# Halved products in the routing of an attention and mixture-of-experts kernel, with its scatters and remainders moved

## The chip, the cores and the metric

One core of one Trainium2 chip runs the whole kernel. The metric is the device time of one execution in microseconds (us); of several executions the median is taken, and less is better. TensorE, VectorE, ScalarE, GpSimd and the DMA queues are PE, DVE, ACT, POOL and SP in the rows.

## What is computed

Linear attention feeds a mixture of experts with one expert a token. Of the reference the parts that matter here:

```python
q_p, k_p = phi(q_s), phi(k_s)                 # exp(h - max(h)), 128 features
kv = np.einsum('bhsm,bhsd->bhmd', k_p, v)     # key sums of a batch
num = np.einsum('bhsm,bhmd->bhsd', q_p, kv)
...
logits = xn @ en.T / tau
expert_idx = np.argmax(logits, axis=1)        # one of 8 experts
...
h = np.maximum(x[mask] @ w1[e], 0.0)
out[mask] = gate_w[mask, None] * (h @ w2[e])
```

There are 8 batches of 576 tokens, 8 heads of 64 numbers, and experts of 512 x 1024 and 1024 x 512 weights.

## The kernel before, in words

The first part, some 210 us, makes attention and routing; the second, the rest, runs 38 steps of 128 tokens through the experts. The change lies in the first part.

Tokens are 36 tiles of 128. A loop (L746) runs over i: it takes keys of tile i and, seven behind, queries of tile i-7, in one round. The order of instructions on every engine is written out by hand (manual_schedule); small jobs are put into named slots of a round (early, spare, mid, ends) and taken out by go() and slot(). In a full round:

- TensorE projects the queries (proj, L374), turns the last tile's query features (qtr, L462) into both banks of tile nuu, projects the keys, adds the keys' products to the key sums (kvmm, L406, one half), makes the numerators (num, L482) into nuu, and adds the other half of kvmm.
- ScalarE copies one half of the turned queries (qcopy, L467) and takes exponentials (feats, L388).
- VectorE copies the other half (qcopy, L469), takes maxima (L378), and reads the numerators out of nuu (num_out, L495 to L501); the next qtr writes nuu only behind that.

nuu is one PSUM tile of two banks of 512 columns; nu[0] and nu[1] are views of it. The numerators use columns 0 to 291 of each bank, the expert logits of the key sums 424 to 487 of the second, the counting products 424 to 455 of the first.

Twice in nine rounds the key sums of a batch are ready (u in 4, 8). Then GpSimd packs them (kv_dense, L424), and two rounds later TensorE turns them (kv_turn, L433, slot spare 3, right ahead of num), VectorE copies them back (kv_turned, L437, slot mid 4), and TensorE multiplies them with the expert embeddings (kv_logits, L444, slot spare 0, right behind num). In the full rounds the turn goes into bank pb[3].

After every third tile routed() handles three tiles: logits are summed, the best expert chosen (sel, L530 to L532, VectorE), tokens before each token counted by products of sel with a triangle and with ones (L537, L539, TensorE), rows worked out (L548 to L558, GpSimd), and the three tiles scattered into expert order (L570, an indirect DMA from GpSimd, one a round, held behind L501 of its round). A table, plan, says in which slot each step stands.

From round 29 on the first expert's weights come in eight pieces; first_split (L608, L610) rounds a piece, and first_rest (L617) subtracts to keep the remainder, on GpSimd.

Of the kernel before, what the change touches and what calls it, by code (L numbers as in the profile page):

```python
# [11 lines left out]
F32 = mybir.dt.float32  # L12
# [5 lines left out]
ALU = mybir.AluOpType  # L18
# [4 lines left out]
P = 128  # L23
B, H, S, D, M = 8, 8, 576, 64, 128
E, F = 8, 1024
# [4 lines left out]
NTILE = NSB * TPS  # L30
G = 3
# [18 lines left out]
SHIFTW = 8  # L50
BESIDE = 554
WARM = 28
FILL1, FILL2, FILL3 = 2, 4, 5
NSTAT = 38
NSTEP = 64
# [9 lines left out]
def attention_moe(ctx: ExitStack, tc: tile.TileContext, qT, kT, v1, omT, emb, tau, w1q, w2q, xs, out):  # L65
    nc = tc.nc
    sync = mybir.DependencyInfo(mybir.DependencyClass.Sync, mybir.DependencyReason.DATA)
# [8 lines left out]
    nuu = ps.tile([P, 2, 512], F32, name="nuu")  # L76
    nu = [nuu[:, a] for a in range(2)]
    pb = [ps.tile([P, 512], F32, name=f"pb{a}") for a in range(4)]
# [9 lines left out]
    one16 = const.tile([P, P], BF16, name="one16")  # L88
# [4 lines left out]
    ident = const.tile([P, P], F32, name="ident")  # L93
    make_identity(nc, ident)

    tri = const.tile([P, P], BF16, name="tri")
# [5 lines left out]
    iotm = const.tile([P, E], F32, name="iotm")  # L102
# [220 lines left out]
    with ExitStack() as c1:  # L323
# [5 lines left out]
        kva, kvs, st = {}, {}, {}  # L329
# [98 lines left out]

        def kv_turn(sb, b):
            kvc = st["kvc", sb, b]  # L430
            st["kvb"] = bank = pb[3] if st["both"] and (sb, b) != (0, 0) else nu[1]
            for c in range(4):
                nc.tensor.transpose(bank[:, c * P : (c + 1) * P], kvc[:, 2 * c : 2 * c + 2, :].rearrange("p a d -> p (a d)"), ident)  # L433

        def kv_turned(sb, b):
            kvt = xgp[NPRE][:, 0:DM].rearrange("p (c m) -> p c m", c=4)
            nc.vector.tensor_copy(kvt.rearrange("p c m -> p (c m)"), st["kvb"])  # L437
            st["kvt", sb, b] = kvt

        def kv_logits(sb, b):  # L440
# [23 lines left out]
        def qcopy(i, s, on_act=False):  # L464
            st["qp", i, s] = qp = p1.tile([P, H, D], F32, name=f"qp{i}_{s}", tag="ftk" if s and not st["both"] and i >= NTILE - LAG else "qp", bufs=3)
            if on_act:
                o = nc.scalar.activation(qp, st["tr", i][s], AF.Copy)  # L467
            else:
                o = nc.vector.tensor_copy(qp, st["tr", i][s])  # L469
            if ("cp", i) in st:  # L470
                tc.declare_no_dep(o.ins, st["cp", i].ins.name, reason="reads the other bank")
            st["cp", i] = o
# [33 lines left out]
        def routed(g):  # L506

            bc = lambda a: a.unsqueeze(2).to_broadcast([P, G, E])
            ibc = lambda a: a.unsqueeze(1).to_broadcast([P, G, E])
            new = lambda n, shape, dt=F32: small.tile(shape, dt, name=f"{n}{g}", tag=n, bufs=1 if n in ("t4", "base") else 2)  # L510
            raw = new("raw", [P, G, E])
            mx = new("mx", [P, G])
            sel = sels[g % 2][:, 0:G]
            lg = st["lg", g]
            fast = g >= NTILE // G - 3
            if fast:
                nc.vector.tensor_reduce(raw, lg.rearrange("p g h e -> p g e h"), axis=AX.X, op=ALU.add)
            else:
                pt = nc.gpsimd.tensor_tensor
                t4 = new("t4", [P, G, 4, E])  # L520
                pt(t4, lg[:, :, 0:4], lg[:, :, 4:8], op=ALU.add)
                pt(t4[:, :, 0:2], t4[:, :, 0:2], t4[:, :, 2:4], op=ALU.add)
                pt(raw, t4[:, :, 0], t4[:, :, 1], op=ALU.add)
            yield
            nc.vector.tensor_reduce(mx, raw, axis=AX.X, op=ALU.max)
            nc.vector.tensor_tensor(raw, raw, bc(mx), op=ALU.subtract)
            yield
            for j in range(G):
                nc.gpsimd.tensor_copy(st["xr", g * G + j][:, DM : DM + E], raw[:, j])
            nc.vector.scalar_tensor_tensor(sel, raw, 0.0, ibc(iotm), op0=ALU.is_ge, op1=ALU.mult)  # L530
            nc.vector.tensor_reduce(mx, sel, axis=AX.X, op=ALU.min)
            nc.vector.tensor_tensor(sel, ibc(iotm), bc(mx), op=ALU.is_equal)  # L532
            yield

            bank, o = nu[0], 424
            pr = bank[:, o : o + (G + 1) * E].rearrange("p (j e) -> p j e", e=E)
            nc.tensor.matmul(pr, tri, sels[g % 2], start=True, stop=False)  # L537
            for j in range(G):
                nc.tensor.matmul(pr[:, j + 1 :], one16, sel[:, j : j + 1].to_broadcast([P, G - j, E]), start=False, stop=j == G - 1)  # L539
            yield  # L540
            base = new("base", [P, G + 1, E])
            rows = base[:, 0:G]
            if fast:
                nc.vector.tensor_tensor(rows, pr[:, 0:G], run.unsqueeze(1).to_broadcast([P, G, E]), op=ALU.add)
                nc.vector.tensor_tensor(run, run, pr[:, G], op=ALU.add)
            else:
                nc.vector.tensor_copy(base, pr)
                pt(rows, rows, run.unsqueeze(1).to_broadcast([P, G, E]), op=ALU.add)  # L548
                pt(run, run, base[:, G], op=ALU.add)
            pos = new("pos", [P, G, 4])  # L550
            if fast:
                nc.vector.tensor_tensor(rows, rows, sel, op=ALU.mult)
                nc.vector.tensor_reduce(pos[:, :, 0], rows, axis=AX.X, op=ALU.add)
            else:
                pt(rows, rows, sel, op=ALU.mult)
                pt(pos, rows[:, :, 0:4], rows[:, :, 4:8], op=ALU.add)
                pt(pos[:, :, 0:2], pos[:, :, 0:2], pos[:, :, 2:4], op=ALU.add)
                pt(pos[:, :, 0:1], pos[:, :, 0:1], pos[:, :, 1:2], op=ALU.add)  # L558
            yield
            if g == GPICK:  # L560
                yield from pick_first()

            posi = new("posi", [P, G], I32)
            (nc.vector if fast else nc.gpsimd).tensor_copy(posi, pos[:, :, 0])
            for j in range(G):
                yield
                if j == 0 and g in DRAINS:
                    tc.add_manual_dep(nc.gpsimd.drain().ins, st["out"].ins.name, sync, reason="idle behind the last scatter")
                xr = st["xr", g * G + j]
                w = nc.gpsimd.indirect_dma_start(  # L570
                    out=xs, out_offset=bass.IndirectOffsetOnAxis(ap=posi[:, j : j + 1], axis=0),
                    in_=xr, in_offset=None, bounds_check=ROWS - 1, oob_is_err=False,
                )
                tc.add_manual_dep(w.ins, st["out"].ins.name, sync, reason="one scatter a tile")
                written(w)

        def pick_first():
# [34 lines left out]
        def first_rest(n):  # L612
            q, (_, h, l) = n // 2, W[("w1", "w2")[n % 2]]
            raw = st["rf", n]
            for c in range(0, F, 256):
                c = slice(c, c + 256)
                nc.gpsimd.tensor_tensor(l[:, 0, q, c], raw[:, c], h[:, 0, q, c].bitcast(F32), op=ALU.subtract)  # L617

        def first_steps():

# [125 lines left out]
        for i in range(NTILE + LAG + 2):  # L746
# [133 lines left out]
            if sums and done % G == G - 1:  # L880
                g = done // G
                steps = routed(g)
                if g == GPICK:
                    plan = [(ends, i), (mid, i + 1, 2), (mid, i + 1, 1), (spare, i + 2, 0), (mid, i + 2, 0)]
                    plan += [(mid, i + 3, 2), (mid, i + 3, 1)] + [(ends, i + 3 + k) for k in range(3)]
                elif g == NTILE // G - 2:
                    plan = [(ends, i), (ends, i + 1), (ends, i + 1), (spare, i + 2, 0), (mid, i + 2, 0), (mid, i + 2, 1)]
                    plan += [(ends, i + 2), (ends, i + 3), (ends, i + 3)]
                elif i >= NTILE:
                    plan = [(ends, i)] * 3 + [(spare, i + 1, 0), (mid, i + 1, 0), (mid, i + 1, 1)]  # L890
                    plan += [(ends, i + 2 + k) for k in range(3)]
                else:
                    plan = [(ends, i), (mid, i + 1, 2), (mid, i + 1, 1), (spare, i + 2, 0), (mid, i + 2, 0)]
                    plan += [(mid, i + 3, 2)] + [(ends, i + 3 + k) for k in range(3)]
                if NTILE - 3 < i < NTILE:
                    plan[-3:] = [(ends, i + 3), (mid, i + 4, 3), (ends, i + 5)]
                for n, (d, *key) in enumerate(plan):
                    todo = at(d, *key) if key[0] < NTILE + LAG + 2 else behind
                    todo.insert(0 if n == 0 else len(todo), (next, steps, None))
# [468 lines left out]
```

## Time and profile before

| | us |
|---|---|
| median of 3 runs | 635.08 |
| the runs | 635.08, 634.54, 641.2 |
| the profiled execution | 639.0 |
| its span | 637.4 |

Granted TensorE clock of the profiled execution: 0.998 of full speed. The profile is of one execution, so sums of its durations stand against 639.0, of which 1.6 lie around the span. A row of the timeline merges equal instructions that follow each other: its second number runs from the start of the first to the end of the last. Ends of matmuls are modelled. Idle time in square brackets stands before the instruction, with what ended it.

### The profile page before, as it was taken

To read this page: it belongs to the slowest core of one execution; us is meant where nothing else is said; L and a number is where in the kernel's file an instruction comes from. 1 tells how busy PE (TensorE), PEld (TensorE's weight loads), DVE (VectorE), ACT (ScalarE), POOL (GpSimd) and SP (SyncE) were. 2 spreads that over 40 slices of the span, in tenths; PEclk is the share of its full clock that TensorE was granted. 3 is DMA by queue.
4 is the path that set the end of the run, shared out by engine and by line. 5 is a ranking of instruction groups with operands and counts; after the bars stand their busy time and mean duration, and the time that the engine had idled before them with its cause. 6 is when DMAs were issued, how large, how long until landed. Compare 5 with 4: busy or idle time off the path is not lost.

```text
span 637.4 us, 19063 instructions
## 1 busy us (share of the span) xinstructions
PE 626.5 (98%) x6289; PEld 534.8 (84%) x6290; DVE 499.4 (78%) x909; ACT 434.5 (68%) x1143; POOL 423.1 (66%) x603
## 2 busy tenths in 40 slices
PE   9999999999999999999999999999999999999996
PEld 8999999988878787888888888888888888888885
DVE  5788888898879846789888798877778787878754
ACT  6989898898998417666666666666575757576640
POOL 3013333455777644569897898879797988797952
PEclk9999999999999999999999999999999999999999
DMA  7755665777782278888869687887878786968631
GB/s 256 216 153 170 210 197 177 226 206 235 250 284 87 101 236 296 249 214 242 244 193 230 208 225 231 201 248 185 242 186 222 216 242 196 234 206 225 195 116 47
DMA packets 143264, 132.20 MB, mean 207 GB/s; under 512 B 107766, under 2 KB 107894, under 8 KB 143168
## 3 DMA queue, kind: packets, MB, share of 16 engines
q1 hardware_dynamic: 136544, 109.96, 61.4%
q0 software_dynamic: 6480, 20.91, 8.4%
q8 instruction: 57, 0.93, 0.6%
q14 instruction: 39, 0.32, 0.2%
q10 hardware_dynamic: 144, 0.07, 0.0%
HBM read 83.78 MB, written 21.97 MB: 166 GB/s over the span
## 4 chain that ended last, share of the span: by engine, by line
PE 70%; ACT 2%; DVE 1%; DMA 1%; issue 0%; POOL 0%; ACTq 0%
PE pb L285 31%; PE po L285 31%; PE pb L374 2%; PE fs_o L285 2%; PE nuu L482 2%; PE fs_a L285 1%; PE pb L267 1%; ACT ftq L388 1%; PE kva L406 1%; DMA qt<-qT 1%; PE pb L462 0%; PE nuu L462 0%; ACT sq L296 0%; DVE xr L501 0%; DVE rt_p L299 0%
## 5 line engine op out<-in xcount | busy, mean ns | idle before, releaser
L240 POOL TENSOR_TENSOR w2l<-raww,w2h 128x256 f32 x128 | 143.6, 1122 | 7.6
L240 POOL TENSOR_TENSOR w1l<-raww,w1h 128x256 f32 (+1 forms) x130 | 114.9, 884 | 14.6 <-DMA xgp<-xs 5.3
L285 PE MATMUL po<-w2h,hh 128*128 (+1 forms) x288 | 112.2, 390 | 0.0
L285 PE MATMUL po<-w2h,hl 128*128 (+1 forms) x288 | 112.1, 389 | 0.0
L285 PE MATMUL po<-w2l,hh 128*128 (+1 forms) x288 | 112.0, 389 | 0.0
L285 PE MATMUL pb<-w1h,xh 128*128 (+1 forms) x280 | 109.4, 391 | 0.1
L285 PE MATMUL pb<-w1h,xl 128*128 (+1 forms) x280 | 109.1, 390 | 0.0
L285 PE MATMUL pb<-w1l,xh 128*128 (+1 forms) x280 | 109.0, 389 | 0.0
L1086 DVE COPY pl<-pb 128x512 uint16<-128x512 uint16 x68 | 46.7, 690 | 55.9 <-ACT pl L1082 53.0
L1082 ACT ACTIVATE pl<-pb 128x512 uint16<-128x512 uint16 x68 | 39.4, 582 | 69.5 <-PE pb L285 61.1
L388 ACT ACTIVATE ftq<-pb,nmq 128x128 f32<-128x128 f32 x288 | 79.7, 432 | 2.2 <-DVE nmq L378 2.2
L388 ACT ACTIVATE ftk<-pb,nmk 128x128 f32<-128x128 f32 x272 | 76.6, 492 | 4.9 <-DVE nmk L378 4.9
L315 POOL DMA_INDIRECT y<-xgp,tail x36 | 44.6, 1240 | 52.0 <-DVE w1h L234 25.3
L1104 DVE COPY wd<-t 128x1024 uint16<-128x1024 uint16 x68 | 67.3, 991 | 1.6 <-DMA t<-pl 1.5
L1120 ACT ACTIVATE hh<-wd 128x1024 fp32r<-128x1024 f32 x34 | 36.1, 1062 | 42.1 <-DVE wd L1104 37.4
L285 PEld LDWEIGHTS po<-w2h,hh 128*128 128x128 f32 x288 | 54.1, 188 | 11.3
L285 PEld LDWEIGHTS po<-w2h,hl 128*128 128x128 f32 x288 | 54.0, 187 | 11.3
L285 PEld LDWEIGHTS po<-w2l,hh 128*128 128x128 f32 x288 | 54.1, 188 | 11.0
L285 PEld LDWEIGHTS pb<-w1h,xl 128*128 128x128 f32 x280 | 52.6, 188 | 11.2 <-DVE xl L269 0.2
L285 PEld LDWEIGHTS pb<-w1h,xh 128*128 128x128 f32 x280 | 52.5, 187 | 11.1 <-ACT tail L1148 0.5
L285 PEld LDWEIGHTS pb<-w1l,xh 128*128 128x128 f32 x280 | 52.6, 188 | 10.8
L1124 DVE SCALAR_TENSOR_TENSOR hl<-wd,hh 128x1024 fp32r<-128x1024 f32 x34 | 54.8, 1611 | 2.9 <-ACT hh L1120 2.3
(342 smaller groups left out, 1257.2 us busy)
## 6 DMA issues: line engine op xcount, KB each, us to landing
raww<-w1q SPq DMA_DIRECT2D x38, 512.0 KB
raww<-w2q SPq DMA_DIRECT2D x38, 512.0 KB
qt<-qT SPq DMA_DIRECT2D x36, 256.0 KB
kt<-kT SPq DMA_DIRECT2D x35, 256.0 KB
xg<-xs SPq DMA_DIRECT2D x23, 260.5 KB
xgp<-xs SPq DMA_DIRECT2D x15, 260.5 KB
rf<-w1q SPq DMA_DIRECT2D x4, 512.0 KB
rf<-w2q SPq DMA_DIRECT2D x4, 512.0 KB
```

The lines of the kernel that those rows point to most:

```text
L240: ils.append(eng.tensor_tensor(at(l, d)[:, c], raw[:, c], at(h, d)[:, c].bitcast(F32), op=ALU.subtract))
L267: nc.tensor.transpose(bank[:, c * P : (c + 1) * P], src[:, o + c * P : o + (c + 1) * P], ident)
L285: done.append(nc.tensor.matmul(dst, x[:, c * P : (c + 1) * P], ws.rearrange("p o f -> p (o f)"), start=(begin and i == 0 and k == 0), stop ...
L315: w = nc.gpsimd.indirect_dma_start(out=out, out_offset=bass.IndirectOffsetOnAxis(ap=(xg[:, DM:] if tail is None else tail)[:, E : E + 1].b ...
L374: nc.tensor.matmul(st["pj" + w, i, a][:, c, :], st[w, i][r, c, :], om[r, :], start=True, stop=True)
L388: nc.scalar.activation(ft[:, h, :], pj[:, h, :], AF.Exp, bias=nm[:, h : h + 1])
L482: nc.tensor.matmul(pn[a][s * D : s * D + D, h, :], st["qp", i, s][:, 2 * h + a, :], kvs[sb, int(u > 4 - s)][:, 4 * a + h, :], start=True, ...
L1082: nc.scalar.activation(planes[1][:, o : o + 512], halved(src)[:, :, 1], AF.Copy)
L1086: nc.vector.tensor_copy(planes[0][:, o : o + 512], halved(src)[:, :, 0])
L1104: nc.vector.tensor_copy(to, src)
L1120: nc.scalar.activation(hh, wd[:, 0:F], AF.Relu)
L1124: nc.vector.scalar_tensor_tensor(hl, wd[:, 0:F], 0.0, hh.bitcast(F32), op0=ALU.max, op1=ALU.subtract)
```

## The change

It has four parts. The turns of key sums (kv_turn) are made of two 64-row halves, eight products of 64 columns for four of 128; one half goes into pb[3], the other into columns 296 to 423 of both banks of nuu (in the first and the last turn into nu[0] and nu[1]), and VectorE copies them in two copies. The counting products are made for 64 tokens' rows at a time, eight for four. A scatter in a full round is held behind VectorE's query copy (moved) and stands in slot mid 4 of the round after. The first remainder of each piece of weights is held behind the last choice of experts (sel).

```diff
+SPARE = 296
...
         def kv_turn(sb, b):
             kvc = st["kvc", sb, b]
-            st["kvb"] = bank = pb[3] if st["both"] and (sb, b) != (0, 0) else nu[1]
+            two = nuu[:, :, SPARE : SPARE + P].rearrange("p k (c r) -> p k c r", r=64)
+            if st["both"] and (sb, b) != (0, 0):
+                one = pb[3][:, 0 : 2 * P].rearrange("p (k c r) -> p k c r", c=2, r=64)
+            else:
+                one, two = (b[:, 0 : 2 * P].rearrange("p (k c r) -> p k c r", c=2, r=64) for b in nu)
+            st["kvb"] = one, two
             for c in range(4):
-                nc.tensor.transpose(bank[:, c * P : (c + 1) * P], kvc[:, 2 * c : 2 * c + 2, :].rearrange("p a d -> p (a d)"), ident)
+                for s, to in enumerate((one, two)):
+                    r = slice(64 * s, 64 * s + 64)
+                    nc.tensor.transpose(to[:, c // 2, c % 2], kvc[r, 2 * c : 2 * c + 2, :].rearrange("p a d -> p (a d)"), ident[r, r])
 
         def kv_turned(sb, b):
             kvt = xgp[NPRE][:, 0:DM].rearrange("p (c m) -> p c m", c=4)
-            nc.vector.tensor_copy(kvt.rearrange("p c m -> p (c m)"), st["kvb"])
+            for s, got in enumerate(st["kvb"]):
+                nc.vector.tensor_copy(kvt.rearrange("p (k c) (s r) -> p s k c r", k=2, r=64)[:, s], got)
...
-                o = nc.vector.tensor_copy(qp, st["tr", i][s])
+                o = st["moved"] = nc.vector.tensor_copy(qp, st["tr", i][s])
...
-            nc.vector.tensor_tensor(sel, ibc(iotm), bc(mx), op=ALU.is_equal)
+            st["sel"] = nc.vector.tensor_tensor(sel, ibc(iotm), bc(mx), op=ALU.is_equal)
...
-            nc.tensor.matmul(pr, tri, sels[g % 2], start=True, stop=False)
+            half = [slice(c, c + 64) for c in range(0, P, 64)]
+            for r in half:
+                nc.tensor.matmul(pr[r], tri[:, r], sels[g % 2], start=True, stop=False)
             for j in range(G):
-                nc.tensor.matmul(pr[:, j + 1 :], one16, sel[:, j : j + 1].to_broadcast([P, G - j, E]), start=False, stop=j == G - 1)
+                for r in half:
+                    nc.tensor.matmul(pr[r, j + 1 :], one16[:, r], sel[:, j : j + 1].to_broadcast([P, G - j, E]), start=False, stop=j == G - 1)
...
-                tc.add_manual_dep(w.ins, st["out"].ins.name, sync, reason="one scatter a tile")
+                tc.add_manual_dep(w.ins, st["moved" if st["both"] else "out"].ins.name, sync, reason="one scatter a tile")
...
-                nc.gpsimd.tensor_tensor(l[:, 0, q, c], raw[:, c], h[:, 0, q, c].bitcast(F32), op=ALU.subtract)
+                o = nc.gpsimd.tensor_tensor(l[:, 0, q, c], raw[:, c], h[:, 0, q, c].bitcast(F32), op=ALU.subtract)
+                if c.start == 0:
+                    tc.add_manual_dep(o.ins, st["sel"].ins.name, sync, reason="not beside the choice of experts")
...
+                for k in range(3):
+                    if i + 4 + k < NTILE:
+                        plan[k - 3] = (mid, i + 4 + k, 4)
```

On TensorE, in a round that turns key sums (kva are the key sums' products, xgp the packed sums, nuu behind them the numerators), the order before is:

```order
L406 MATMUL kva_0_1_887<-vt10v,ftk_1_928 64x65 x7
L433 MATMUL pb_74<-ident,xgp_141 128x128 [waits DVE_49,Activation_49,Pool_49]
L433 MATMUL pb_74<-ident,xgp_141 128x128 x3
L482 MATMUL nuu<-kvs_0_440,qp_0_980 64x73 [waits DVE_49]
L482 MATMUL nuu<-kvs_0_440,qp_1_978 64x73
```

and after:

```order
L407 MATMUL kva_0_1_892<-vt10v,ftk_1_933 64x65 x7
L441 MATMUL pb_74<-ident,xgp_141 128x64 [waits DVE_49,Activation_49,Pool_49]
L441 MATMUL nuu<-ident,xgp_141 128x64 [waits DVE_49]
L441 MATMUL pb_74<-ident,xgp_141 128x64
L441 MATMUL nuu<-ident,xgp_141 128x64
L441 MATMUL pb_74<-ident,xgp_141 128x64
L441 MATMUL nuu<-ident,xgp_141 128x64
L441 MATMUL pb_74<-ident,xgp_141 128x64
L441 MATMUL nuu<-ident,xgp_141 128x64
L491 MATMUL nuu<-kvs_0_440,qp_0_985 64x73 [waits DVE_49]
L491 MATMUL nuu<-kvs_0_440,qp_1_983 64x73
```

The turn stands where it stood. Both rows of the first numerator name VectorE's semaphore; counted out in the programs as built, the count waited for is that of query copy L469 before (in the first row's round and in the five others like it), and that of the second key-sum copy (L446) after.

On GpSimd, in the round in which key sums are packed (raw are logits less their maximum, the scatter's source is a finished tile xr, base the counts), before:

```order
L529 COPY xr_1294<-raw_1311 128x8
L570 DMA xs<-xr_807,posi_1284 38016x576 [waits DVE_49]
L424 COPY xgp_141<-kvs_0_1396 128x2x4x64 [waits PE_49,Activation_49]
L490 COPY xr_1559<-ids 128x1 [waits DMASW0_49]
L548 TENSOR_TENSOR base_1576<-base_1576,run 128x24 [waits DVE_49]
```

and after:

```order
L538 COPY xr_1308<-raw_1325 128x8
L425 COPY xgp_141<-kvs_0_1407 128x2x4x64 [waits PE_49,Activation_49]
L582 DMA xs<-xr_812,posi_1298 38016x576 [waits DVE_49]
L499 COPY xr_1577<-ids 128x1 [waits DMASW0_49]
L548 TENSOR_TENSOR base_1576<-base_1576,run 128x24 [waits DVE_49]
```

The scatter changes places with the packing alone; otherwise it keeps its place in GpSimd's queue and waits there longer. In rounds 31 to 41 the four remainders of a piece go ahead of the scatter in the same way.

## Rows read from the trace of the kernel before

**Rows 1.** The page: engines (busy us, share of the span, instructions).

```profile
PE 626.5 (98%) x6289; PEld 534.8 (84%) x6290; DVE 499.4 (78%) x909; ACT 434.5 (68%) x1143; POOL 423.1 (66%) x603
```

**Rows 2.** Waits of ACT from 45 to 180: total us, times, longest.

```profile
ACT qp L467 <- PE nuu L462: 12.0, 11, 2.4
```

**Rows 3.** Timeline, 90 to 98.5: start, us, engine, line, operation, [idle before <-releaser].

```profile
91.45 1.28 DVE L378 TENSOR_REDUCE nmk<-pb 128x4 f32<-128x512 f32 x2
...
92.06 0.66 PE L433 MATMUL pb<-ident,xgp 128*128 128x128 f32 x4
...
92.65 1.25 PE L482 MATMUL nuu<-kvs,qp 128*64 128x73 f32 x32
...
92.83 0.69 DVE L437 COPY xgp<-pb 128x512 f32<-128x512 f32 x1
...
94.44 0.17 DVE L495 TENSOR_SCALAR rr<-nuu 128x8 f32<-128x8 f32 x1 [0.62 <-PE nuu L444]
...
95.62 0.22 DVE L450 COPY kvs<-nuu 128x64 f32<-128x64 f32 x1
...
95.89 0.71 PE L462 MATMUL nuu<-ident,ftq 64*128 64x64 f32 x16
...
95.98 0.98 POOL L570 DMA_INDIRECT xs<-xr,posi  x1 [1.65 <-DVE sel L530]
...
96.43 1.11 PE L374 MATMUL pb<-om,kt 64*128 64x128 f32 x16
...
97.35 0.60 ACT L467 ACTIVATE qp<-nuu 128x512 f32<-128x512 f32 x1 [2.40 <-PE nuu L462]
```

**Rows 4.** Timeline, 62.2 to 68.4, a round with a scatter at its turn of queries.

```profile
62.24 0.99 POOL L570 DMA_INDIRECT xs<-xr,posi  x1 [1.57 <-DVE sel L530]
...
62.44 0.66 PE L462 MATMUL nuu<-ident,ftq 64*128 64x64 f32 x16
...
63.70 0.60 ACT L467 ACTIVATE qp<-nuu 128x512 f32<-128x512 f32 x1 [1.05 <-PE nuu L462]
...
65.72 0.19 PE L537 MATMUL nuu<-sel,tri 128*128 128x32 bf16 x1
65.76 0.22 PE L539 MATMUL nuu<-sel,one 128*128 128x24 bf16 x3
...
66.10 0.15 DVE L495 TENSOR_SCALAR rr<-nuu 128x8 f32<-128x8 f32 x1
```

**Rows 5.** Timeline, 145 to 154, another such round and the copy after it.

```profile
145.79 0.71 PE L462 MATMUL nuu<-ident,ftq 64*128 64x64 f32 x16
...
147.25 0.60 ACT L467 ACTIVATE qp<-nuu 128x512 f32<-128x512 f32 x1 [2.31 <-PE nuu L462]
...
151.06 0.70 PE L462 MATMUL nuu<-ident,ftq 64*128 64x64 f32 x16
...
152.68 0.72 ACT L467 ACTIVATE qp<-nuu 128x512 f32<-128x512 f32 x1
```

**Rows 6.** Timeline, 69 to 73.2, another round that turns key sums.

```profile
69.62 1.04 POOL L570 DMA_INDIRECT xs<-xr,posi  x1 [0.54 <-issue]
...
70.18 0.66 PE L433 MATMUL pb<-ident,xgp 128*128 128x128 f32 x4
...
71.09 0.69 DVE L437 COPY xgp<-pb 128x512 f32<-128x512 f32 x1 [0.30 <-PE pb L433]
...
72.61 0.17 DVE L495 TENSOR_SCALAR rr<-nuu 128x8 f32<-128x8 f32 x1 [0.82 <-PE nuu L444]
```

**Rows 7.** Timeline, 150 to 200, POOL alone: the remainders of one piece.

```profile
165.12 2.79 POOL L617 TENSOR_TENSOR w2l<-rf,w2h 128x256 fp32r<-128x256 f32 x4
```

**Rows 8.** Timeline, 107 to 113, a scatter behind the turn's end.

```profile
107.14 0.60 ACT L467 ACTIVATE qp<-nuu 128x512 f32<-128x512 f32 x1 [0.46 <-PE nuu L462]
...
107.38 1.00 POOL L570 DMA_INDIRECT xs<-xr,posi  x1 [0.49 <-DVE nmq L378]
...
108.35 1.28 DVE L378 TENSOR_REDUCE nmk<-pb 128x4 f32<-128x512 f32 x2
```

## The prediction

> **What bounds the kernel now.** I read the engines first: TensorE is busy for 98% of the span [rows 1], so over the whole program nothing else can be the limit. But the change touches only the first part, and there the share hides much: between two products of a chain TensorE is counted busy with work that could have been done at another time. So I went on to the waits of ScalarE in that part. Its query copy waited for the turn of queries (L462) eleven times, 12.0 us in all, the longest 2.4 us [rows 2]. An engine that sits idle so long with nothing ahead of it is not what sets the pace; what comes before it is. The timeline shows what that is, and I read it around the rounds that turn key sums.
>
> In such a round one chain goes through three engines: the numerators at 92.65, the logits of key sums, VectorE's reading of the numerators from 94.44 on, the copy of the logits at 95.62, the next turn of queries at 95.89, and then ScalarE's query copy at 97.35, after 2.40 us of idle time [rows 3]. Every step stands right behind the one before it: L450 ends at 95.62 + .22 = 95.84 and L462 starts .05 later. Whatever delays the numerators in this round delays ScalarE by as much, and from there the next round. That is the stage from which the first part of the change has to be read.
>
> The second thing that the timeline shows is a hold. When a scatter is running on GpSimd as the turn of queries ends, the query copy starts not at that end but a little behind the scatter's: scatter 62.24 + .99 = 63.23, turn 62.44 + .66 = 63.10, copy 63.70 [rows 4]; 95.98 + .98 = 96.96, turn 96.60, copy 97.35 [rows 3]; a turn at 145.79 + .71 = 146.50 has its copy at 147.25 [rows 5]. Six turns stand so, the first in rows 5, with copies .41 to .89 behind the turn, 3.9 us in all; where no scatter runs at the end the copy is there at once. TensorE is not held: its key projections start at 96.43 inside the scatter of 95.98 [rows 3].
>
> **Turns of key sums: a new wait, +6.6.** Of the eight turns six are in full rounds. Before, the turn wrote pb[3] alone, and the numerators behind it went on at once: turn 92.06 + .66 = 92.72, numerators from 92.65, VectorE's copy of the turned sums from 92.83 beside them [rows 3]. Now half of the turn lies in columns of nuu, the tile that the numerators write, and the first numerator waits for VectorE's second copy out of it. The copy that lay beside TensorE's work comes onto its path. Queued behind the first numerator are all of TensorE's products: the rest of the numerators, the logits, the second half of the key sums' products, the next projections.
>
> How long: VectorE is busy with maxima until 91.45 + 1.28 = 92.73 [rows 3]. The turn ends no later: sixteen products of its new shape take .70 [rows 5], eight about .35 to .45, so 92.5 at the latest. The copies thus start at about 92.75. One of 128x512 takes .69, one of 128x64 .22 [rows 3]; on a straight line between them 128x256 costs .22 + .47 x 192/448 = .42, two .84. They end at 93.59, and the first numerator comes .05 behind, as L462 behind L450: 93.64 for 92.65, 1.0 us late. Three rounds are of this kind. In the other three a scatter ends as the turn does (69.62 + 1.04 = 70.66, turn 70.18 + .66 = 70.84), and VectorE comes only at 71.09 [rows 6]; that third scatter of a group stays where it is. There the copies end at 71.09 + .84 = 71.93, the numerators start at 71.98, and VectorE reads them 1.79 later, as 94.44 stands to 92.65 [rows 3]: 73.77 for 72.61 [rows 6], 1.2 late. Together 3 x 1.0 + 3 x 1.2 = 6.6.
>
> No row shows a copy of that size. If two cost no more than the one (.69), it is 6 x .15 less: 5.7. If each costs as much as the whole (1.38), 6 x .54 more: 9.8. The two turns outside full rounds only get two copies for one: 2 x .15 = +.3.
>
> **Scatters behind the query copy, -1.7.** The scatter now starts once VectorE's copy has ended, about 1.0 us behind the copy's start, and no longer covers the end of a turn. All 3.9 us of hold may go; but a copy that comes earlier helps only if what it leads to can come earlier too. TensorE went on during the hold, so in four of the six rounds the next reading of the numerators is tied to TensorE and gains about .1: in rows 5 it is at 66.10, right behind the counting products' end at 65.76 + .22 = 65.98. In two rounds more comes back: in rows 6 the copy of the following round is at 152.68 while its turn ended at 151.06 + .70 = 151.76, so ScalarE and not TensorE was late there and up to .75 of its lateness is the hold's; in the other, by the same reading, .5. That is .4 + .75 + .5 = 1.7. The ends are 0 and -3.9.
>
> On GpSimd the scatters start later by .6 to .8 (the first of a group) or some 2.4 (the second). What stands behind them in its queue is the index copy and, a round later, the counts; neither is wanted within a us. The source tiles come free later, but they are a ring of seven. SP's queue is not touched.
>
> A page of the Trainium skill speaks against this part: "SBUF — State Buffer", section "SBUF: two separate sides", says that only VectorE and GpSimd share a port pair and that ScalarE never waits on another engine. By it ScalarE's late copies would have another cause than the scatter. The rows show ScalarE's copy .39 to .47 behind the scatter's end [rows 3, 4]; they do not show why. If the page is right about this place, moving the scatter is worth nothing.
>
> **Counting products, 0.** Four products at 65.72 to 65.98 [rows 4] become eight half as wide, in twelve groups. If eight take half of the sixteen's .70 [rows 5], .35 for .26, it is 12 x .09 = +1.1. If the halves run two at a time and the change of shape on either side goes, up to the .1 between their end and 66.10 [rows 4] comes back: -1.2. Between ends of like size I take 0.
>
> **Remainders and packing ahead of the scatter, 0.** Four remainders take 2.79 us on GpSimd [rows 7]; this engine is off the path (66% busy [rows 1]), and the weights are wanted only after routing. If the scatters behind them meet a turn again, up to +1; if the choice of experts was slowed by them, -.5.
>
> **The sum.** 6.6 + .3 - 1.7 = +5.2. Against the profiled execution, 639.0 (637.4 and 1.6 around it), it gives 644.2. That execution was 3.9 above the median of the runs; the terms come from single waits and not from its surplus, so they stand on 635.1 as well: 640.3.
>
> **Rivals.**
>
> *The new wait costs nothing (not slower).* The numerators' delay falls into time that the next round has to wait anyway, or is caught up by the round after. For it: a turn of queries and not a wait of its own is what ScalarE names in its idle time [rows 2]. Against it: that turn itself stands .05 behind the chain [rows 3]. Then 640.3 - 6.6 = 633.7, and with the whole hold gone 631.5.
>
> *The scatter holds something else (slower).* At its new place it runs from 1.0 to 2.0 behind the start of the query copies. If it holds back the end of the key projections as it held the turn's, VectorE's maxima of keys start at 2.4 instead of 1.2 behind the copy (108.35 for 107.14 [rows 8]) and end at 3.7; the numerators are then read at 3.7 for 2.4 (66.10 for 63.70 [rows 4]) where nothing else was late, or for 3.1 where something was, some .9 a round on the mean. Up to fifteen rounds have a scatter at the new place; in half of them it is +6.7, 647.0. It decides from two rounds on. Against it: in rows 7 a scatter to 108.38 lay over the end of such projections, and the maxima came at 108.35; but VectorE had other work until then.
>
> *The scatter is not the cause of the late copies.* Then the hold stays, and the time is 640.3 + 1.7 = 642.0. By the page named above this is what would happen. For the scatter as the cause: the three cases above share the distance to its end, while the distance to the turn's end changes.
>
> **How the numbers follow.** Forecast .54, own range 637.5 to 643.5 (copies at 5.7 to 9.8, hold 0 to -3.9, counting +-1.1, taken together and not all at their ends). No cost of the new wait .26; scatter holds the projections .12; scatter not the cause .08. One per cent, 6.35 us, is about what a measurement of this kernel can tell from no change. Faster than 628.7 needs the first rival, the whole hold and the counting's gain: a quarter of .26, .07. Slower than 641.4: three tenths of the forecast (.16), all but a little of the second rival (.11), and half of the last and a little (.05): .32. Within: .61. The range goes from 631.0, under which about .09 lies, to 646.5, over which half of the second rival and a little of the forecast lie.
>
> **What would show it.** Right: in six rounds the first numerator stands .05 behind VectorE's second key-sum copy, at 128x256 near .42 each, TensorE idle about 1 us ahead of it, and ScalarE's wait in the round after is longer by as much; scatters start behind the query copies, and these stand right behind the turn of queries. Wrong: numerators at their old distance from the turn; or the wait is there and ScalarE's wait behind it is no longer than 2.4; or copies still late behind a turn with no scatter near; or maxima of keys idle behind a scatter's end.

## The result, and the profile after

The changed kernel has a median of 640.22 us in 21 runs (638.73 to 644.06), the kernel before 634.77 in 21 runs (633.76 to 641.2). The ratio is 1.0084 with a 95% interval of 1.0071 to 1.0097: some 5.3 us slower, less than one per cent. The forecast was 640.3. The total came out almost to the tenth; the terms behind it did not, and the runs below take them apart.

The page of the changed kernel, engines, for [rows 1]:

```profile
PE 620.8 (97%) x6369; PEld 531.2 (83%) x6370; DVE 498.6 (78%) x917; ACT 434.8 (68%) x1143; POOL 423.5 (66%) x603
```

TensorE shows 5.7 us less than in [rows 1]. That is not less work, nor is it the change: a second profile of the kernel before (below) has

```profile
PE 621.6 (98%) x6289; PEld 531.1 (84%) x6290; DVE 496.4 (78%) x909; ACT 435.2 (69%) x1143; POOL 422.9 (67%) x603
```

so the sums of two executions of one kernel differ by 4.9, and the waits have to be read one by one. TensorE's and VectorE's waits between 45 and 180, total us, times and longest, with ScalarE's that answers to [rows 2], in the changed kernel:

```profile
ACT qp L476 <- PE nuu L471: 16.8, 14, 2.6
DVE rr L504 <- PE nuu L453: 9.7, 6, 1.8
PE nuu L491 <- DVE xgp L446: 5.6, 5, 1.1
```

The third line is the new wait: the numerators (L491) behind the key-sum copies (L446). The view lies over five of the six turns in full rounds, and 5.6 / 5 is 1.1 us each. ScalarE's wait for the turn of queries has grown, as has VectorE's for the key sums' logits (L453; 4.4 us before), since both stand behind the numerators. The timeline of the round that answers to [rows 3] (start, duration, instruction; idle time in brackets):

```profile
91.32 1.28 DVE L379 TENSOR_REDUCE nmk<-pb 128x4 f32<-128x512 f32 x2
...
91.92 0.27 PE L441 MATMUL pb<-ident,xgp 64*128 64x64 f32 x1
...
92.52 0.42 DVE L446 COPY xgp<-pb 128x256 f32<-128x256 f32 x1
...
92.97 0.42 DVE L446 COPY xgp<-nuu 128x256 f32<-128x256 f32 x1
...
93.45 1.25 PE L491 MATMUL nuu<-kvs,qp 128*64 128x73 f32 x32 [1.08 <-DVE xgp L446]
...
95.17 0.17 DVE L504 TENSOR_SCALAR rr<-nuu 128x8 f32<-128x8 f32 x1 [1.47 <-PE nuu L453]
...
96.62 0.71 PE L471 MATMUL nuu<-ident,ftq 64*128 64x64 f32 x16
...
97.38 0.60 ACT L476 ACTIVATE qp<-nuu 128x512 f32<-128x512 f32 x1 [2.54 <-PE nuu L471]
```

The first numerator stands 1.53 behind the turn's start; it stood .59 behind it. A copy of 128x256 takes .42, as the straight line had it, and the numerator comes .06 behind the second one's end (92.97 + .42 = 93.39). The chain behind it is the old one and .9 later up to the turn of queries, which starts 4.70 behind the key sums' turn for 3.83; ScalarE's copy is only .2 later, since the one in [rows 3] was late already. And the other round, for [rows 6]:

```profile
70.58 0.41 DVE L446 COPY xgp<-pb 128x256 f32<-128x256 f32 x1
...
71.03 0.42 DVE L446 COPY xgp<-nuu 128x256 f32<-128x256 f32 x1
...
71.50 1.25 PE L491 MATMUL nuu<-kvs,qp 128*64 128x73 f32 x32 [1.14 <-DVE xgp L446]
...
73.22 0.17 DVE L504 TENSOR_SCALAR rr<-nuu 128x8 f32<-128x8 f32 x1 [1.77 <-PE nuu L453]
```

Here the copies were expected at .91 behind the turn's start, where [rows 6] had VectorE's; they stand .68 behind it (the turn starts at 69.90). A scatter lies over the turn's end here too (69.53 to 70.58), and in this execution it does not delay them. For [rows 4], a round whose scatter is moved and whose choice is counted:

```profile
62.55 0.66 PE L471 MATMUL nuu<-ident,ftq 64*128 64x64 f32 x16
...
63.25 0.60 ACT L476 ACTIVATE qp<-nuu 128x512 f32<-128x512 f32 x1 [0.50 <-PE nuu L471]
...
64.32 0.99 POOL L582 DMA_INDIRECT xs<-xr,posi  x1 [2.95 <-DVE qp L478]
...
65.63 0.18 PE L548 MATMUL nuu<-sel,tri 128*64 128x32 bf16 x2
...
65.66 0.24 PE L551 MATMUL nuu<-sel,one 128*64 128x24 bf16 x6
...
66.01 0.17 DVE L504 TENSOR_SCALAR rr<-nuu 128x8 f32<-128x8 f32 x1 [0.18 <-ACT ftq L389]
```

ScalarE's copy is .04 behind the turn's end (63.21), and the scatter starts .96 behind VectorE's copy start (63.36). Eight counting products take .27 from first start to last end, as four took .26. So far every step looks as forecast, the scatters' too. That the gain from the scatters is an illusion came out with the first experiment.

### The profile page after: what moved, and what is told of

Read it like the earlier page. It is cut to its first block, busy times and chain, and to the rows that moved or that the text cites. A ratio compares the mean times of both kernels' runs of the same rounds, so it can differ in the third digit from the quotient of the medians.

```text
span 637.4 us, 19226 instructions
## 1 busy us (share of the span) xinstructions
PE 620.8 (97%) x6369; PEld 531.2 (83%) x6370; DVE 498.6 (78%) x917; ACT 434.8 (68%) x1143; POOL 423.5 (66%) x603
## 4 chain that ended last, share of the span: by engine, by line
PE 68%; DVE 2%; ACT 2%; DMA 1%; issue 0%; POOL 0%; ACTq 0%; DVEq 0%
PE pb L286 31%; PE po L286 30%; PE fs_o L286 2%; PE pb L375 2%; PE nuu L491 1%; PE fs_a L286 1%; PE pb L268 1%; ACT ftq L389 1%; PE kva L407 1%; DMA xgp<-xs 1%; DMA qt<-qT 1%; PE pb L471 0%; PE nuu L471 0%; DVE nmq L379 0%; ACT wd L1123 0%
## 5 line engine op out<-in xcount | busy, mean ns | idle before, releaser
L582 POOL DMA_INDIRECT xs<-xr,posi x36 | 36.4, 1010 | 37.5 <-DVE qp L478 25.0
```

What stands on the lines that cost most here:

```text
L582: w = nc.gpsimd.indirect_dma_start(out=xs, out_offset=bass.IndirectOffsetOnAxis(ap=posi[:, j : j + 1], axis=0), in_=xr, in_offset=None, bo ...
```

## The experiments

Twelve runs, in three series of four on three chips; each is compared with runs of the kernel before on its own chip. Their median was 634.96 in the first series, 635.0 in the second and 639.27 in the third. "First part" is the time from the first query copy of ScalarE (L467 in before) to its last, in the run's one profile, and the length of a round below is the time from one such copy to the next; for the changed kernel it is 185.02, for the first profile of before 183.7.

| run | median, us | ratio to before (95%) | first part, us |
|---|---|---|---|
| before_again | 634.79 | 0.9995 (0.9984 to 1.0005) | 180.54 |
| kv_only | 645.5 | 1.0160 (1.0136 to 1.0183) | 186.47 |
| kv_undone | 633.97 | 0.9984 (0.9973 to 0.9996) | 179.28 |
| kv_cols | 638.38 | 1.0057 (1.0038 to 1.0075) | 182.56 |
| scatter_undone | 640.74 | 1.0098 (1.0061 to 1.0134) | 185.41 |
| scatter_only | 638.08 | 1.0046 (1.0017 to 1.0075) | 179.79 |
| count_only | 635.62 | 1.0006 (0.9988 to 1.0025) | 179.99 |
| kv_only_again | 642.84 | 1.0113 (1.0065 to 1.0161) | 186.70 |
| kv_swap | 642.32 | 1.0056 (1.0039 to 1.0074) | 186.33 |
| kv_split | 646.55 | 1.0128 (1.0096 to 1.0159) | 191.10 |
| scatter_only_again | 640.64 | 1.0023 (0.9997 to 1.0048) | 187.37 |
| rest_no_rem | 641.56 | 1.0034 (1.0011 to 1.0057) | 187.67 |

**A second profile of the kernel before.** No edit.

> The kernel before, once more, for a second profile. First theory (the prediction): the six late query copies are in every execution, 3.9 us in all, and the profiled execution's surplus of 3.9 over the median lies elsewhere. Rival: that surplus is the late copies themselves, chance of that one execution; then they come to under 2 us here and the span is near 633.

The profiled execution took 634.89 us. The timeline around the turn of queries that answers to [rows 3]:

```profile
93.96 0.71 PE L462 MATMUL nuu<-ident,ftq 64*128 64x64 f32 x16
...
94.05 0.99 POOL L570 DMA_INDIRECT xs<-xr,posi  x1 [1.65 <-DVE sel L530]
...
94.71 0.60 ACT L467 ACTIVATE qp<-nuu 128x512 f32<-128x512 f32 x1 [1.59 <-PE nuu L462]
```

The scatter lies over the turn's end exactly as in [rows 3], .09 behind its start, and the copy is there .04 behind that end (94.67), long before the scatter's (95.04). None of the six copies is late. Even in the first profile a scatter did not hold every turn: one turn ended at 129.66 under a scatter that ran to 130.15, and ScalarE's copy stood at 129.78. The rival holds: the late copies belong to the execution that the prediction was worked out from, and 3.2 of its 4.1 us over this one lie in the first part (183.7 against 180.54), .9 ahead of it. What the prediction took off for the scatters, 1.7 us, was not there to be won in a usual execution.

**The turn alone, and all but the turn.** kv_only is the kernel before with this hunk alone; kv_undone is the changed kernel without it:

```diff
-            st["kvb"] = bank = pb[3] if st["both"] and (sb, b) != (0, 0) else nu[1]
+            two = nuu[:, :, SPARE : SPARE + P].rearrange("p k (c r) -> p k c r", r=64)
...
+            for s, got in enumerate(st["kvb"]):
+                nc.vector.tensor_copy(kvt.rearrange("p (k c) (s r) -> p s k c r", k=2, r=64)[:, s], got)
```

> The kernel before with the turn of key sums in halves and nothing else of the change. First theory: the new wait costs all of its terms, 6.6 + .3 = +6.9 us, ratio 1.011, with six numerators .05 behind the second key-sum copy. Rival (the wait falls into time that the next round loses anyway): under +2 us, ratio under 1.003.

> The changed kernel with the turn of key sums as before, in one bank and one copy. First theory: what is left is the hold, -1.7 (0 to -3.9), so ratio .997 (.994 to 1.000). Rival (the scatter at its new place, the counting or the remainders cost time): ratio over 1.000, up to 1.005. If the new wait costs nothing the ratio stays at that of the whole change, 1.008.

With the turn alone the first part is 5.9 longer than in before_again, and the wait is not absorbed. The median is more than that above, 10 us; where these come from is taken up below. Without the turn the change is 1.0 us faster than the kernel before (0.3 to 1.7 by the interval), and its first part 1.26 shorter. 5.93 - 1.26 = 4.67 stands against 4.48 for the whole change: the parts add up. kv_undone lies in the range of its first theory (.994 to 1.000), but not by the late copies that this theory takes away, which are not there in before_again.

**Other ways to turn and copy.** Three edits of the changed kernel. kv_cols makes the halves of columns and keeps out of nuu:

```diff
+                for a in range(2):
+                    nc.tensor.matmul(bank[a * D : a * D + D, c * P : (c + 1) * P], kvc[:, 2 * c + a, :], ident, start=True, stop=True)
```

> The changed kernel with the turn in halves of columns: eight products of 64 columns of the packed sums against the whole identity, all into pb[3], one copy; no half lies in nuu, so the numerators wait for no copy. First theory: as the changed kernel with the turn as before, within .5 us, ratio .997, since only the wait cost anything. Rival (the half-shaped turn itself is dear, or gains by the shape that its neighbours have): over 1 us to either side of that kernel.

```profile
91.00 1.09 PE L435 MATMUL pb<-ident,xgp 128*64 128x128 f32 x16
...
91.90 1.22 PE L484 MATMUL nuu<-kvs,qp 128*64 128x73 f32 x32
...
92.23 0.69 DVE L439 COPY xgp<-pb 128x512 f32<-128x512 f32 x1 [0.47 <-PE pb L435]
```

The numerators wait for nothing, .90 behind the turn's start, but the turn takes 1.09 for .66: the eight products written as matmuls are sixteen instructions (x16). The six rounds are .26 longer on the mean than in kv_undone, 1.6 in all, so the first theory's "within .5" falls, and the rival (the turn itself is dear) holds for this form. Another 1.8 is one round of this profile that waits for keys and weights to land; whether it is in every execution is not known.

kv_swap turns the order of the two copies round:

```diff
-            for s, got in enumerate(st["kvb"]):
+            for s, got in reversed(list(enumerate(st["kvb"]))):
```

> The changed kernel with the order of the two key-sum copies turned round: the half in nuu is copied first, the half in pb[3] second. First theory (the numerators wait for the copy out of nuu alone): they start one copy earlier, .45 in each of six rounds, 2.7 less than the changed kernel, about 637.5, ratio 1.004; in the timeline the first numerator stands 1.1 behind the turn's start instead of 1.5. Rival (the time goes to the shape of the turn or to the copies themselves, whatever their order): as the changed kernel, 1.008.

```profile
42.53 0.27 PE L441 MATMUL pb<-ident,xgp 64*128 64x64 f32 x1
...
43.13 0.42 DVE L446 COPY xgp<-nuu 128x256 f32<-128x256 f32 x1
...
43.61 1.25 PE L491 MATMUL nuu<-kvs,qp 128*64 128x73 f32 x32 [0.62 <-DVE xgp L446]
43.66 0.42 DVE L446 COPY xgp<-pb 128x256 f32<-128x256 f32 x1
```

The first numerator is 1.08 behind the turn's start and runs beside the second copy: one copy's time earlier than the 1.54 of the same round of the changed kernel. The ratio, 1.0056 for 1.0084, moved the way foretold, but by .0028 and not by .0044 (1.004), and on a chip with more delays, below: three of the six rounds are .32 to .46 shorter than in the changed kernel, and in the other three a scatter makes the first copy .68 or .69 late and they take 7.28 to 7.33 for 7.25. It is the copy out of nuu that the numerators wait for, not copies as such.

kv_split copies the half in nuu bank by bank:

```diff
-                nc.vector.tensor_copy(kvt.rearrange("p (k c) (s r) -> p s k c r", k=2, r=64)[:, s], got)
+                for k in range(2) if isinstance(got, list) else [slice(0, 2)]:
+                    nc.vector.tensor_copy(to[:, k], got[k] if isinstance(got, list) else got)
```

> The changed kernel with the half in nuu copied bank by bank, in two copies of 128x128 for one of 128x256. First theory: on the line between the copies measured (.22 at 64 columns, .42 at 256) they cost about .29 each, so the numerators wait .15 longer in each of six rounds, +.9, ratio 1.010; the first bank's numerators still wait for the last copy. Rival (numerators wait only for copies out of their own bank, or the wait is absorbed): no more than the changed kernel.

```profile
42.66 0.42 DVE L448 COPY xgp<-pb 128x256 f32<-128x256 f32 x1
...
43.12 0.49 DVE L448 COPY xgp<-nuu 128x128 f32<-128x128 f32 x2
...
43.66 1.06 PE L493 MATMUL nuu<-kvs,qp 128*64 128x73 f32 x26 [1.15 <-DVE xgp L448]
```

(The view ends at 44.5 and cuts the last row.) The two small copies take .49 for .42, and the first numerator is 1.60 behind the turn's start (42.06) for 1.54: it waits for the last copy. So the wait grows with the copies, by .06 and not by the .15 that I had worked out, since the second one starts .21 behind the first. The ratio is .7% over that of kv_swap in the same series, 4.6 us where these steps (.46 + .06 in six rounds) explain 3.1. Another 1.4 us is in one round of this profile: a scatter (69.72 to 70.77) makes the copies .67 late and the wait 1.67, and behind it TensorE's clock is down (stretches of 2 us; the engines stand in the order PE, its weight loads, DVE, ACT, POOL, and PEclk is the third number from the end).

```profile
70.00:72.00 2.00, 0.46 (x8) 0.35 (x8) 1.60 (x5) 2.00 (x9) 1.09 (x3) 1.00 0.75 232
72.00:74.00 2.00, 1.78 (x34) 1.78 (x36) 0.16 (x1) 1.08 (x5) 0.00 (x0) 0.63 0.16 65
74.00:76.00 2.00, 2.00 (x38) 1.88 (x36) 0.91 (x4) 0.00 (x0) 0.23 (x1) 0.52 0.00 0
```

So the new wait can cost more than its own length.

**Scatters, counting and remainders one by one.** scatter_undone is the changed kernel with the old name and place of the scatters' wait, scatter_only and count_only are the kernel before with these hunks alone:

```diff
-                tc.add_manual_dep(w.ins, st["out"].ins.name, sync, reason="one scatter a tile")
+                tc.add_manual_dep(w.ins, st["moved" if st["both"] else "out"].ins.name, sync, reason="one scatter a tile")
...
+                for k in range(3):
+                    if i + 4 + k < NTILE:
+                        plan[k - 3] = (mid, i + 4 + k, 4)
```

> The changed kernel with its scatters where they stood before. First theory (a scatter over the end of a turn delays the query copies by chance of the execution, and only at the old place): with the new wait most executions are held, so about 645, ratio 1.013 to 1.017, and where the profile shows copies late behind scatters they make up the difference to 640. Rival (the place of the scatters is worth nothing): as the changed kernel, 1.008.

> The kernel before with the scatters moved and nothing else. First theory: usual executions of the kernel before have no late copies, so nothing is gained, ratio .999 to 1.001. Rival (the prediction's term, -1.7 of late copies): .997. If the new place delays the maxima of keys: over 1.003.

> The kernel before with the counting products in halves and nothing else. First theory: the 1.0 us that the whole change without its turn gained is theirs, ratio .9985, with some .1 us less in each round that counts. Rival (the prediction's term, 0): .9995 to 1.0005, and then the gain is that of the scatters or the remainders.

scatter_undone is 1.0098, where the whole change is 1.0084: the scatters' place is worth some .4 us in the first parts of these two profiles (185.41 to 185.02), and no copy is late. The first theory, that the new wait brings the late copies back, finds nothing in the profile, and the ratio stands by the rival's 1.008, though its interval (1.0061 to 1.0134) just reaches 1.013. Counting alone cannot be told from the kernel before (1.0006), as the prediction had it and against the first theory of this run, though its first part is .55 shorter. Scatters alone were slower, by the size of the last theory (over 1.003) but without its delayed maxima: their profile was the fastest of twelve executions (633.41, first part .75 shorter than before_again), ten of the others lay at 634.7 to 642.4 and the last at 643.9. Something that the profile had not caught cost the ten 1 to 9 us. Two more profiles were taken for that: scatter_only_again, and rest_no_rem, which is the changed kernel with the old turn and without

```diff
-                if c.start == 0:
-                    tc.add_manual_dep(o.ins, st["sel"].ins.name, sync, reason="not beside the choice of experts")
```

> The kernel before with the scatters moved, once more: its profile was its fastest execution (633.4), the others lay at 635 to 644 with clocks of .990 to .999. First theory (in some executions TensorE waits for the second part's weights or tokens near 295, its clock falls for some us, 4 us in all, and the first part is the same in all): a profile near 638 shows this wait and clock and a first part of 179.8 from the first query copy to the last; if it is a chance of that series, the median is back near 634.5. Rival: near 638 the first part is longer, by late copies or maxima.

> The changed kernel with the turn as before and the remainders not held behind the choice of experts: scatters and counting products alone. First theory (remainders cost and give nothing, the prediction's 0): as the changed kernel with the turn as before, .998, first part 179.3. Rival (holding them gives or costs something): over .5 us to either side in the rounds from 31 to 41.

Both caught it, in the same place, and not near 295, where the first theory of scatter_only_again had it. rest_no_rem, timeline around the last choice of experts but two:

```profile
193.67 1.00 POOL L574 DMA_INDIRECT xs<-xr,posi  x1 [0.16 <-issue]
...
194.69 3.32 DVE L533 TENSOR_TENSOR sel<-iotm,mx 128x24 bf16<-128x24 f32 x1
...
195.20 2.76 POOL L621 TENSOR_TENSOR w2l<-rf,w2h 128x256 fp32r<-128x256 f32 x4
...
198.06 0.24 PE L540 MATMUL nuu<-sel,tri 128*64 128x32 bf16 x2 [2.49 <-DVE sel L533]
```

and its stretches of 2 us (busy time by engine as above, then PEclk, DMA share and GB/s):

```profile
196.00:198.00 2.00, 0.00 (x0) 0.00 (x0) 2.00 (x2) 0.00 (x0) 2.00 (x4) 0.91 0.57 230
198.00:200.00 2.00, 1.94 (x13) 1.17 (x12) 1.97 (x6) 1.36 (x6) 0.10 (x1) 0.50 0.00 0
200.00:202.00 2.00, 2.00 (x21) 2.00 (x22) 1.76 (x9) 0.82 (x4) 0.75 (x1) 0.50 0.00 0
202.00:204.00 2.00, 2.00 (x38) 1.88 (x36) 1.87 (x3) 1.08 (x4) 0.45 (x2) 0.50 0.37 133
204.00:206.00 2.00, 2.00 (x27) 1.51 (x25) 1.07 (x5) 2.00 (x8) 0.00 (x0) 0.88 0.03 8
```

The last of the three steps that choose an expert, .18 us elsewhere, lasts 3.32: it starts as GpSimd begins a train of small copies and the four remainders, and ends with them. TensorE has nothing to do for 2.49 us, and then its granted clock is .50, the lower of its two levels (1.2 GHz), from 198 to 204. In scatter_only_again the same step takes 3.31 at 194.41 and TensorE waits 2.48. The rounds that hold it are 4.5 us longer than in kv_undone and 3.8 longer than in scatter_only; most of the rest of these long first parts are the delays of the third chip, below. By the Trainium skill, page "SBUF — State Buffer", section "Who interferes with whom", a VectorE instruction with two inputs in SBUF and a GpSimd instruction that reads SBUF use one port pair, and one of them blocks for the whole of the other; these two traces agree, 3.32 and 3.31 for .18, with the addition that the step was blocked by a whole train of instructions and not by one. But meeting the train is not enough. In before_again the same instructions stand in the same order and at the same distances, and nothing is blocked:

```profile
191.29 0.25 POOL L490 COPY xr<-ids 128x1 int32<-128x1 int32 x1
191.31 0.19 DVE L532 TENSOR_TENSOR sel<-iotm,mx 128x24 bf16<-128x24 f32 x1
...
191.81 2.81 POOL L617 TENSOR_TENSOR w2l<-rf,w2h 128x256 fp32r<-128x256 f32 x4
```

In scatter_only the first small copy and the step both start at 190.72, and the step takes .18. What brings the block in one execution and not in another stays open. In the six profiles of kernels with the remainders held behind the choice the steps take .75 at most, kv_swap and kv_split on this chip among them; in the six others without the hold, .76. By its order the hold should end a block before the four remainders, so that the fourth part of the change looks like a companion of the second; that the moved scatter has a part in the block is likely by the clocks alone. On the third chip the kernel before stays at .998 or more in 23 executions, where seven of scatter_only_again's ten and eight of rest_no_rem's ten lie under that, and in the second series scatter_only has .990 to .997 in the ten executions above 635 and .998 and .999 in the two below. The hold alone was not run, and rest_no_rem and kv_undone, which differ by it, ran on different chips, so what it is worth was not measured; the rival of rest_no_rem (over .5 us in these rounds) fits with that reserve.

**The surplus of the turn alone.**

> The kernel before with the turn of key sums in halves, once more, for a profile of another execution: the first one's profile was its fastest execution, 640.9, and the others lay at 642 to 646. First theory: near 645 its profile shows query copies late behind scatters as the first profile of the kernel before did, 3 to 5 us in all, and near 641 it shows none. Rival: near 645 no late copies, and the time is lost elsewhere (the second part, or a load that lands late).

The profiled execution took 644.34, its first part 186.70, as in kv_only, and no copy is late: the rival holds. The second part has become longer, by 3.3 us against before_again (430.4 for 427.1, from the last query copy on). Its timeline and stretches near 295:

```profile
295.27 0.50 PE L286 MATMUL pb<-w1h,xh 128*128 x1 [0.26 <-POOL w1l L241]
...
297.66 0.50 PE L286 MATMUL pb<-w1h,xl 128*128 x1 [1.65 <-DVE xl L1132]
```

```profile
298.00:300.00 2.00, 2.00 (x7) 1.57 (x6) 1.97 (x3) 0.32 (x3) 1.79 (x2) 0.57 1.19 247
300.00:302.00 2.00, 2.00 (x7) 1.56 (x6) 1.91 (x4) 0.12 (x1) 0.28 (x1) 0.58 0.92 288
```

TensorE waits .26 us for GpSimd's remainder of the weights (w1l) and 1.65 for VectorE's remainder of a token tile (xl), and again the granted clock is down to near half behind the wait. kv_cols' profile, also its slowest execution, has the same (.47 and 1.66, then .50). In kv_only's first profile (640.92) the wait in this place is .61 and the clock stays up; in before_again there is none, in the changed kernel .26. Why it comes in some executions and not in others stays open.

**Delays on the third chip.** Its four profiles have late reads behind scatters, .36 to .69 us behind the end of what they read, in five to nine places each between 70 and 180; none of the eight profiles of the first two series has one over .2. Only one in each is at a query copy, since the scatters have moved; the others are at what now lies under them. scatter_only_again:

```profile
86.38 1.20 PE L483 MATMUL nuu<-kvs,qp 128*64 128x73 f32 x32
...
86.57 1.04 POOL L571 DMA_INDIRECT xs<-xr,posi  x1 [0.16 <-DVE nmq L379]
...
88.17 0.17 DVE L496 TENSOR_SCALAR rr<-nuu 128x8 f32<-128x8 f32 x1 [0.60 <-PE nuu L483]
```

The numerators end at 87.58, the scatter at 87.61, and VectorE reads at 88.17; in scatter_only, with a scatter in the same place, it reads .12 behind the numerators' end. On this chip the kernel before had a median of 639.27, and the first profile of before, with its six late copies, took 639.0. The distance to the scatter's end is alike too: the late reads on this chip start .41 to .65 behind it, and in the first profile of before five of the six query copies .39 to .48. That it is the same thing was not shown, as no profile of before was taken there, and why a read waits for a scatter stays open.

## Why the prediction was right, and where it was not

The forecast (slower by 5.2, within one per cent) came true at 5.3. The mechanism of its largest term is right; that the total agrees to the tenth is luck, as the terms show.

- **The new wait, +6.6: right, and its size within a sixth.** Six rounds took 43.60 us (7.34, 7.25, 7.27, 7.25, 7.25, 7.25) for 37.91 in before_again (6.48, 6.28, 6.33, 6.28, 6.27, 6.28), 5.7 or .95 each, and nothing of it was absorbed, so the rival that let it cost nothing is out. The three plain rounds lost .93 on the mean for 1.0. The three others lost .97 for 1.2, because the late start that [rows 6] shows is of the same kind as the late copies, and a usual execution has none.
- **First and last turn, +.3: about +.1.** The first round's period is 4.97 for 4.86; in the last there is no loss.
- **Scatters, -1.7: wrong in its ground.** The step that failed is "All 3.9 us of hold may go": the hold was in the one profiled execution and not in a usual one. What the first part of scatter_only gained is .75, in two rounds that the prediction never spoke of (.47 and .40), and count_only gains the same .47 in the first of them, so it is not the scatters' alone. I had set the surplus of the profiled execution, 3.9 over the median, aside with the words that the terms "come from single waits and not from its surplus"; the waits of this term were that surplus, to 3.2 us. (Where the prediction says rows 5 for the reading at 66.10, rows 6 for the copy at 152.68 and rows 7 for the scatter to 108.38, the rows are in [rows 4], [rows 5] and [rows 8].)
- **The second rival (the scatter holds something else): right as a mechanism, elsewhere.** On the third chip reads behind scatters are late by .36 to .69, of the numerators and the key sums rather than of the maxima of keys. In the profile of the changed kernel there is none of it.
- **The third rival (the scatter is not the cause): out as a cause, near in its consequence.** Late reads do stand behind scatters and moved with them on the third chip, but only in some executions; in the others the move is worth little, as this rival had it.
- **Counting, 0: right** by the time (1.0006), with .55 in the first part.
- **Remainders, 0: not measured alone.** In no profile of the kernel before did the remainders block the choice, so there holding them had nothing to give. The cover that I named, an engine off the path, was not the point: where they met the choice GpSimd's work blocked VectorE's, which the prediction had at .5 us and the two traces have at 3.1 for the step.

So the total was met because -1.7 for late copies that were not there stood close to -1.26 of gains from other causes. In the first part 5.7 + .1 - 1.26 = 4.5 came of the forecast's 5.2, and the profiles show it (185.02 for 180.54). The other .8 of the 5.3 is in no profile: the second parts are 426.9 for 427.1, and the profiled execution of the changed kernel, 639.06, lies 1.2 under its median. Where it is lost stays open.

## What to carry to other kernels

Before a spare corner of a tile is used, ask who waits on the whole tile: the columns were disjoint, but the next writer of nuu waited for the last reader of them, and the order of two copies was worth .46 us in a round. Take a profiled execution that lies above the median as a warning about its waits: a wait that you mean to remove has to be in a second profile before it counts. And when work moves on GpSimd, look at which VectorE instructions with two inputs in SBUF it will lie beside; a step of .18 us can last as long as the train that it meets.

## What was not expected of the hardware

A scatter of 1.0 us on GpSimd delayed the other engines' reads of TensorE's results by .2 to .9 us in some executions and on one chip in every profile, and not at all in others with the same instructions in the same place (97.35 in [rows 3] against 94.71 in before_again). And waits of 1.65 to 2.49 us on TensorE were followed by a granted clock of .50 to .63 for some 4 to 6 us, in the first part of three profiles and in the second part of two, though not each time: kv_split's waits of 1.68 and 1.64 in two other rounds were not. The changed kernel's waits of 1.1 us, six times over, left the clock where it was.
